# A gated recurrence and a two-branch maximum network: blocks 2 and 3 taken through the seven-product second layer, with the gates and scans of blocks 4 and 5 moved ahead

## The chip, the cores and the metric

The kernel runs on one core of a Trainium2 chip. A core has a matrix engine (TensorE, "PE" in the profile), a vector engine (VectorE, "DVE"), an activation engine (ScalarE, "ACT"), GpSimd ("POOL") and SyncE ("SP"). Each has its own instruction stream, runs it in order, and waits on semaphores for the others. The metric is the device time of one execution in microseconds (us), and lower is better.

## The reference

Four sequences of 6144 steps with 256 channels go through a gated recurrence; its output goes through a layer that takes the larger of two linear maps, and through an output matrix.

```
sig = 1 / (1 + exp(-f_logit))
f = lower_bound + (1 - lower_bound) * sig
i = 1 - f
for t in range(S):                      # S = 6144, batch 4, D = 256
    h = f[:, t] * h + i[:, t] * x[:, t]
    y[:, t] = h
...
h1 = y @ w1                             # 256 -> 1024
h2 = y @ w2
g = maximum(h1, h2)
out = g @ w_out                         # 1024 -> 256, float32
```

The kernel uses max(h1, h2) = h1 + relu(h2 - h1): the first layer is one product with the difference of the weights, and y @ (w1 @ w_out) joins the second layer as two more rows of 128 (the matrix called w13).

## The kernel before

**Tiles.** The 24576 tokens are cut into 48 blocks of 512 (TB), two blocks make a pair p (blocks 2p and 2p+1), so there are 24 pairs (NPAIR). Channels lie on the 128 partitions, in two halves (KC). Blocks 0 to 3 are loaded as they stand and turned on TensorE; from block 4 on, each pair is one chunk of 1024 tokens, which GpSimd's queue casts to 16 bits into a scratch in memory and SyncE's queue reads back transposed (`cross`, L143, which also issues the loads of the next chunk).

**One block's work.** A gate (sigmoid, ACT: L201 for blocks 1 to 3, L279 for the later ones), on DVE the decay (L207), the drive (L217) and two scans (L224), each scan starting from the block before. Then the first layer (`first_layer(j, fc)`, L424): eight groups, fc = 0 to 7, of two matmuls of 512 columns (L434). Two groups fill one dT tile; there are two dT tiles (`ps_d`, bufs=2), and after every second group ACT empties one with a relu into the block's r tiles (L442). These r tiles also hold y.

**Second layer, two forms.** The direct form (`second_layer(j, slot)`, L458) has 40 matmuls of 256 columns a block, issued in eight pieces of five (L480); after every 20 of them a copy (L489) moves the result out of PSUM. The seven-product form (`sevenths(p)`, L517) treats the two blocks of a pair as a 2 by 2 matrix of parts and makes the pair's result out of seven products in place of eight, each of 20 matmuls of 128 columns (L643). Its left sides are r tiles or one of four sums of r tiles (`sum1` to `sum4`, L499, on DVE), its right sides are parts of the output weights or their differences t1 to t4. The products go into PSUM banks called X, B and E; between them a bank is copied into another one (`seed`, L543), saved to memory on chip (`snapshot`, L549), or emptied into the output tile, by an ACT copy (L559) or by a DVE addition with a snapshot (`leave`, L561).

**Order.** It is written out by hand (L657 on), and each engine's stream follows it. Before the change, blocks 0 to 3 use the direct form, and the steps after the start are:

- the first layer of block 2 beside the direct second layer of block 1, one piece a group, with the decay, drive and scans of block 3 in between (L747);
- `cross(6)`; then the first layer of block 3 beside the direct second layer of block 2, with the gates, decays, drives and first scans of blocks 4 and 5 (L762);
- a loop over the pairs from pair 2 (PAIR0) on. It has 16 slots, one first-layer group each. In pair 2, seven slots also take a direct piece of block 3, and one more piece follows in slot 1 of pair 3. From slot 2 of pair 3 (LAG), each slot takes 8.75 of the 140 matmuls (NSEV) of the pair before. The gates of the next pair stand at slots 4, 6, 12 and 14; sums, decays, drives and scans at places counted in ninths of a slot (`seq`).

What is left of the queue follows the loop, and the last pair has a form of its own.

Of the kernel before, what the change touches and what calls it, by code (L numbers as in the profile page):

```python
# [18 lines left out]
def kernel(  # L19
# [10 lines left out]
    nc = tc.nc  # L30

    B, S, D = x.shape
# [6 lines left out]
    LAG = 2  # L39
# [193 lines left out]
    def scan_steps(j):  # L233
        new_mid(j, ("ff", "v"))
        u, ff, v = (mids[j, t] for t in ("u", "ff", "v"))
        new_block(j)
        return [
            lambda: decay(ff, u, slice(0, TB)),
            lambda: drive(v, u, turned[j, 1], slice(0, TB)),
            lambda: scan(j, 0, ff, v, 0),  # L240
            lambda: scan(j, 1, ff, v, 0),
        ]
# [219 lines left out]
    def second_layer(j, slot):  # L462
        ns = TB // P
        n = KC + FC
        total = ns * n
        for k in range(slot * total // FC, (slot + 1) * total // FC):
            i, s = divmod(k, n)
            g, r = divmod(i, 2)
            if s == 0 and r == 0:
                acc["ps"] = ps_o.tile([P, 2, D], FP32, name="ps")  # L470
                if i == 0:
                    acc["osb"] = opool.tile([P, TB // P, D], FP32, name="osb")
            ps, osb = acc["ps"], acc["osb"]
            toks = slice(i * P, (i + 1) * P)
            if s < KC:
                left, right = y_of(j, s)[:, i:TB:ns], w13[:, s, :]
            else:
                fc = s - KC
                left, right = rts[j, fc // KH][:, fc % KH, toks], wob[:, fc, :]
            nc.tensor.matmul(  # L480
                ps[:, r, :],
                lhsT=left,
                rhs=right,
                start=(s == 0 and r == 0),
                stop=(s == n - 1 and r == 1),
                skip_group_check=True,
            )
            if r == 1 and s == n - 1:
                (nc.scalar.copy if j in (0, 3) else nc.vector.tensor_copy)(  # L489
                    out=osb[:, 2 * g : 2 * g + 2, :], in_=ps[:]  # L490
                )
                if i == ns - 1:
                    store(j, osb)
# [17 lines left out]
    def sum1(p):  # L511
        sum_of(p, 1, quarter(p, 1, 0), quarter(p, 1, 1), ALU.add)
# [4 lines left out]
    def sevenths(p):  # L517
# [6 lines left out]
        def product(b, left, w, fresh=False, groups=range(TB // P)):  # L524
            for i in groups:
                for k in range(KH + 1):
                    new = fresh and i == groups[0] and k == 0
                    steps.append([b, left, w(k), i, k, new, None])

        def then(fn):  # L530
            steps[-1][-1] = fn
# [8 lines left out]
        def seed(b, src):  # L540
            def go():
                open_bank(b)
                nc.scalar.copy(out=bank[b][:], in_=bank[src][:])  # L543
            return go
# [8 lines left out]
        def leave(b, j, cols, name, last):  # L553
            def go():
                if j not in osbs:
                    osbs[j] = opool.tile([P, TB // P, D], FP32, name="osb")
                dst = osbs[j][:, :, cols]
                if name is None:
                    nc.scalar.copy(out=dst, in_=bank[b][:])  # L559
                else:  # L560
                    nc.vector.tensor_tensor(  # L561
                        out=dst, in0=bank[b][:], in1=snap[name][:], op=ALU.add
                    )
                if end:
                    store(j, osbs[j], cols=cols)
                elif last:
                    store(j, osbs[j])
            return go
# [25 lines left out]
        def part(t, k2):  # L594
            return lambda: rts[2 * p + t, k2]

        def plain(k2, cols):
            a, b = right(k2, cols)
            return lambda k: a[:, k, :] if k < KH else b

        def given(t):
            return lambda k: t[:, k, :]

        product("X", part(0, 0), plain(0, lo), True)
        then(seed("B", "X"))
        product("E", sub(1), given(t1), True)
        then(snapshot("E", 5))
        if end:
            product("B", part(0, 1), plain(1, lo), groups=range(1))
            product("X", sub(2), given(t2))  # L610
            then(snapshot("X", 2))
            product("B", part(0, 1), plain(1, lo), groups=range(1, 4))
            then(leave("B", ja, lo, None, False))
            product("X", sub(3), given(t3))
            then(leave_both("X"))
            product("E", sub(4), plain(1, hi))
            then(leave("E", ja, hi, 2, True))
            product("X", part(1, 1), given(t4), groups=range(2))
            then(leave_last(slice(0, 2)))
            for i in (2, 3):  # L620
                product("Y", part(1, 1), given(t4), True, groups=range(i, i + 1))
                then(leave_last(slice(i, i + 1)))
        else:
            product("X", sub(2), given(t2))
            then(snapshot("X", 2))
            product("B", part(0, 1), plain(1, lo))
            then(leave("B", ja, lo, None, False))
            product("X", sub(3), given(t3))
            then(leave("X", jb, hi, 5, False))
            product("E", sub(4), plain(1, hi))  # L630
            then(leave("E", ja, hi, 2, True))
            product("X", part(1, 1), given(t4))
            then(leave("X", jb, lo, None, True))
# [23 lines left out]
    with tc.manual_schedule():  # L657
# [85 lines left out]
        turn(turn_steps(3))  # L743
        gate(3)
        cross(5)
        early = scan_steps(3)
        for fc in range(FC):  # L747
            first_layer(2, fc)
            second_layer(1, fc)
            if fc < 4:  # L750
                early[fc]()
        cross(6)
        scans = {PAIR0: pair_scans(PAIR0)}
        gates = {0: 0, 1: 1, 4: 2, 5: 3}
        order = {
            2: ("decay0", "drive0"),
            3: ("scan00",),
            4: ("scan01",),
            6: ("decay1",),
            7: ("drive1",),  # L760
        }
        for fc in range(FC):  # L762
            first_layer(3, fc)
            second_layer(2, fc)
            if fc in gates:
                pair_gate(PAIR0, gates[fc])
            for t in order.get(fc, ()):
                scans[PAIR0][t]()

        queue, due = [], 0  # L770
        pieces3, piece = (1, 3, 5, 9, 11, 13, 15), 0
        for p in range(PAIR0, NPAIR):
            first = p == PAIR0
            more = p + 1 < NPAIR
            seq = [
                (27, scans[p]["scan10"]),
                (36, scans[p]["scan11"]),
                (112, lambda: sum3(p)),
            ]
            if more:  # L780
                scans[p + 1] = pair_scans(p + 1)
                seq += [
                    (64, scans[p + 1]["decay0"]),
                    (66, scans[p + 1]["drive0"]),
                    (70, scans[p + 1]["scan00"]),
                    (84, scans[p + 1]["scan01"]),
                    (131, scans[p + 1]["decay1"]),
                    (133, scans[p + 1]["drive1"]),
                ]
            if not first:  # L790
                seq += [
                    (9, lambda: sum1(p - 1)),
                    (18, lambda: sum2(p - 1)),
                    (50, lambda: sum4(p - 1)),
                ]
                queue += sevenths(p - 1)
            seq.sort(key=lambda e: e[0])
            gates = {4: 0, 6: 1, 12: 2, 14: 3} if more else {}
            for slot in range(2 * FC):
                first_layer(2 * p + slot // FC, slot % FC)  # L800
                if first and slot in pieces3 or p == PAIR0 + 1 and slot == 1:
                    second_layer(2 * PAIR0 - 1, piece)
                    piece += 1
                if p > PAIR0 + 1 or (p == PAIR0 + 1 and slot >= LAG):
                    due += NSEV / (2 * FC)
                    while due >= 1:
                        due -= 1
                        queue.pop(0)()
                if slot == 2 and p + 3 < NPAIR:
                    cross(blocks[2 * p + 6][3])  # L810
                if slot in gates:
                    pair_gate(p + 1, gates[slot])
                while seq and seq[0][0] < (slot + 1) * 9:
                    seq.pop(0)[1]()
# [38 lines left out]
```

## Time and profile before

| | |
|---|---|
| Median of four runs | 378.9 us (378.23 to 379.26) |
| The profiled execution | 379.36 us, of which the span of instructions is 377.6 us |
| Granted TensorE clock in it | 0.998 |
| First layer, L434 | 768 matmuls, mean 379 ns of one |
| Relu evictions, L442 | 192, mean 1023 ns of one |
| Direct second layer, L480 | 160 matmuls of 256 columns, mean 273 ns |
| Seven products, L643 | for 22 pairs, 140 matmuls of 128 columns each, mean 219 ns of one |
| Sums on DVE, L499 | 88, mean 1479 to 1488 ns |
| Copies of the direct form, L489 | 4 on DVE, mean 685 ns; 4 on ACT, mean 588 ns |

Matmuls are pipelined: the mean time of one contains the way through the array, and the distance from one start to the next is shorter. In a timeline, each row gives the start, the time from the first start to the last end of the merged instructions, and the instruction with its output and inputs. The relu evictions, too, overlap a little when they follow each other directly. "Span" is from the first to the last instruction; some time of an execution lies around it.

### The profile page before, as it was taken

The page shows a single profiled execution, that of the slowest core. Times are in us where ns is not written, and L with a number is a line of the kernel's source. Part 1 is how long each engine was busy: PE and PEld are TensorE (multiplying, and loading weights), DVE is VectorE, ACT ScalarE, POOL GpSimd, SP SyncE. Part 2 cuts the span into 40 slices and gives each one's busy share as a digit, 9 for nine tenths or more (in the row PEclk, how much of TensorE's full clock was granted, in tenths as well). Part 3 has the DMA queues.
Part 4 walks back from the last instruction along what each step waited for, and adds up shares of the span by engine and source line. Part 5 has one row for each costly group of instructions (what it writes and reads, how often), then busy time and mean ns, then how long its engine had stood idle before and what let it go on. Part 6 is the DMA issues. An engine that isn't in the chain of part 4 may idle for free.

```text
span 377.6 us, 9634 instructions
## 1 busy us (share of the span) xinstructions
PE 368.3 (98%) x4156; PEld 280.4 (74%) x4156; DVE 338.2 (90%) x408; ACT 303.1 (80%) x412; POOL 41.3 (11%) x80
## 2 busy tenths in 40 slices
PE   7799999999999999999999999999999999999995
PEld 5577767777777777777777777777777777777784
DVE  5696789999999999999999999999999999999762
ACT  5856798888888798888888887987988888888752
POOL 1401101110120201210101101202011101000000
PEclk9999999999999999999999999999999999999999
DMA  7999999999998989989999999899999989960223
GB/s 270 237 194 246 223 166 187 221 231 205 278 182 169 269 147 251 272 165 221 228 191 260 199 193 264 123 242 266 158 240 272 199 200 273 144 249 2 114 113 112
DMA packets 104543, 77.17 MB, mean 204 GB/s; under 512 B 93298, under 2 KB 95348, under 8 KB 103796
## 3 DMA queue, kind: packets, MB, share of 16 engines
q1 hardware_dynamic: 101536, 51.19, 59.8%
q0 software_dynamic: 2544, 25.17, 34.8%
q8 instruction: 32, 0.52, 0.6%
q10 hardware_dynamic: 420, 0.20, 0.2%
q14 instruction: 11, 0.09, 0.1%
HBM read 53.48 MB, written 48.23 MB: 269 GB/s over the span
## 4 chain that ended last, share of the span: by engine, by line
PE 94%; DMA 4%; SPq 0%; POOL 0%; DVE 0%; issue 0%; ACT 0%; DVEq 0%
PE ps L643 45%; PE dT L434 43%; PE ps L480 5%; DMA xT<-in_x_dram 2%; DMA r<-in_moe_w_dram 1%; PE ps L174 1%; SPq L117 0%; POOL wob L666 0%; DVE osb L561 0%; POOL fT L105 0%; DVE osb L582 0%; ACT sn L574 0%; PE dT L643 0%; POOL waited L341 0%; DVEq L561 0%
## 5 line engine op out<-in xcount | busy, mean ns | idle before, releaser
L442 ACT ACTIVATE r<-dT 128x1024 f16<-128x1024 f32 x192 | 195.9, 1023 | 53.5 <-PE dT L434 53.3
L434 PE MATMUL dT<-r,wd 128*128 128x512 f16 x768 | 225.0, 379 | 0.0
L643 PEld LDWEIGHTS <-S 128*128 128x128 f16 x1760 | 115.5, 101 | 37.2 <-DVE S L499 0.2
L643 PEld LDWEIGHTS <-r 128*128 128x128 f16 x1320 | 90.9, 101 | 36.8 <-issue 0.2
L224 DVE TENSOR_TENSOR_SCAN r<-ff,r,v 128x512 f16<-128x512 f16 x88 | 108.2, 1271 | 0.8
L643 PE MATMUL ps<-t,S 128*128 128x128 f16 x1320 | 101.6, 219 | 0.0
L499 DVE TENSOR_TENSOR S<-r 128x2560 f16<-128x2560 f16 x44 | 65.5, 1488 | 15.2 <-ACT r L442 15.2
L434 PEld LDWEIGHTS <-wd 128*128 128x128 f16 x768 | 67.6, 113 | 4.7 <-DVE wd L358 0.2
L643 PE MATMUL ps<-wob,r 128*128 128x128 f16 x704 | 69.9, 219 | 0.0
L499 DVE TENSOR_TENSOR S<-r,S 128x2560 f16<-128x2560 f16 x44 | 65.1, 1479 | 0.0
L279 ACT ACTIVATE u<-fT 128x512 f16<-128x512 f16 x88 | 56.1, 638 | 0.0
L341 POOL CAST waited<-fT 128x1 f32<-128x1 f16 x22 | 15.6, 707 | 278.4 <-DMA fT<-scr 278.4
L207 DVE TENSOR_SCALAR ff<-u,nom 128x512 f16<-128x512 f16 (+1 forms) x98 | 31.8, 347 | 8.5 <-ACT u L201 3.1
L643 PE MATMUL ps<-w,r 128*128 128x128 f16 x176 | 38.5, 219 | 0.0
L643 PE MATMUL ps<-t,r 128*128 128x128 f16 x430 | 34.1, 219 | 0.1
L561 DVE TENSOR_TENSOR osb<-ps,sn 128x512 f32<-128x512 f32 x44 | 30.1, 685 | 3.2 <-PE ps L643 3.2
L643 PE MATMUL ps<-wob,S 128*128 128x128 f16 x352 | 32.6, 219 | 0.0
L217 DVE TENSOR_TENSOR v<-u,xT 128x1024 f16<-128x1024 f16 x44 | 30.2, 686 | 0.0
L549 ACT COPY sn<-ps 128x512 f32<-128x512 f32 x44 | 25.8, 586 | 2.0 <-PE ps L643 2.0
L559 ACT COPY osb<-ps 128x512 f32<-128x512 f32 x43 | 25.1, 583 | 0.8 <-PE ps L643 0.8
L480 PEld LDWEIGHTS <-r 128*128 128x128 f16 x160 | 16.0, 101 | 6.5
L643 PE MATMUL ps<-w,S 128*128 128x128 f16 x88 | 19.3, 219 | 0.0
(58 smaller groups left out, 133.3 us busy)
## 6 DMA issues: line engine op xcount, KB each, us to landing
out_dram<-osb SPq DMA_DIRECT2D x46, 512.0 KB, 3.8
scr<-in_f_logit_dram POOLq DMA_DIRECT2D x22, 512.0 KB, 7.6
scr<-in_x_dram POOLq DMA_DIRECT2D x22, 512.0 KB, 10.3
r<-in_moe_w_dram SPq DMA_DIRECT2D x4, 512.0 KB, 6.4
fT<-in_f_logit_dram POOLq DMA_DIRECT2D x3, 256.0 KB, 8.7
xT<-in_x_dram POOLq DMA_DIRECT2D x3, 256.0 KB, 9.4
out_dram<-osb SPq DMA_DIRECT2D x3, 256.0 KB, 2.5
osb<-in_f_logit_dram SPq DMA_DIRECT2D x2, 256.0 KB, 3.4
```

What stands on the lines that cost most here:

```text
L207: nc.vector.tensor_scalar(out=ff[:, h, cols], in0=u[:, h, cols], scalar1=nom[:, h : h + 1], scalar2=1.0, op0=ALU.mult, op1=ALU.add,)
L217: nc.vector.tensor_tensor(out=like(v[:, :, cols], xT), in0=like(u[:, :, cols], xT), in1=xT, op=ALU.mult,)
L224: nc.vector.tensor_tensor_scan(out=y_of(j, h), data0=ff[:, h, o : o + TB], data1=v[:, h, o : o + TB], initial=0.0 if t0 == 0 else y_of(j - ...
L279: nc.scalar.activation(out=mids[p + NBLK, "u"][:, h, cols], in_=held[c, 0][:, h, cols], func=AF.Sigmoid, scale=-1.0,)
L434: nc.tensor.matmul(dT[:, fc % 2, :], lhsT=wd[:, kc, unit_cols(fc)], rhs=y_of(j, kc), start=(kc == 0), stop=(kc == KC - 1),)
L442: nc.scalar.activation(out=rts[j, k][:, g - 1 : g + 1, :].rearrange("p q (i m) -> p q i m", m=P), in_=dT[:].rearrange("p q (m i) -> p q i ...
L480: nc.tensor.matmul(ps[:, r, :], lhsT=left, rhs=right, start=(s == 0 and r == 0), stop=(s == n - 1 and r == 1), skip_group_check=True,)
L499: nc.vector.tensor_tensor(out=t[:], in0=a, in1=b, op=op)
L549: nc.scalar.copy(out=t[:], in_=bank[b][:])
L559: nc.scalar.copy(out=dst, in_=bank[b][:])
L561: nc.vector.tensor_tensor(out=dst, in0=bank[b][:], in1=snap[name][:], op=ALU.add)
L643: nc.tensor.matmul(bank[b][:, i, :], lhsT=a[:, k, cols], rhs=w, start=fresh, stop=after is not None, skip_group_check=True,)
```

## The change

Blocks 2 and 3 (pair 1) leave the direct form and go through the seven products:

- In the first layer of block 2, the eight direct pieces of block 1 come one group later (so that piece 7 falls into the first layer of block 3), block 3's scans come all ahead of it, and the gates 0 to 2 of pair 2 and its first decay, drive and scans are placed there.
- The first layer of block 3 has that one direct piece, and gate 3 of pair 2. Behind it stand sum 3 of pair 1, and the second decay and drive of pair 2.
- In the pair loop, pair 2 now has the seven products of pair 1 from slot 2 on, and sums 1, 2 and 4 of pair 1. The direct pieces in the loop are gone. In pair 2 alone, gates 0 and 1 of the next pair are one slot later, and its first decay, drive and scans one slot (nine ninths) later.
- For pair 1 alone, product X is not seeded into bank B but saved as a snapshot, bank B is opened afresh by its own product, and the two are added on DVE as B leaves.
- Both copies of block 1's direct form go from DVE to ACT.

```diff
@@ second_layer
             if r == 1 and s == n - 1:
-                (nc.scalar.copy if j in (0, 3) else nc.vector.tensor_copy)(
+                nc.scalar.copy(
                     out=osb[:, 2 * g : 2 * g + 2, :], in_=ps[:]
                 )
@@ sevenths
+        begin = p == PAIR0 - 1
         product("X", part(0, 0), plain(0, lo), True)
-        then(seed("B", "X"))
+        then(snapshot("X", 1) if begin else seed("B", "X"))
         product("E", sub(1), given(t1), True)
...
-            product("B", part(0, 1), plain(1, lo))
-            then(leave("B", ja, lo, None, False))
+            product("B", part(0, 1), plain(1, lo), begin)
+            then(leave("B", ja, lo, 1 if begin else None, False))
@@ the order
         cross(5)
-        early = scan_steps(3)
+        for step in scan_steps(3):
+            step()
+        scans = {PAIR0: pair_scans(PAIR0)}
         for fc in range(FC):
             first_layer(2, fc)
-            second_layer(1, fc)
-            if fc < 4:
-                early[fc]()
+            if fc:
+                second_layer(1, fc - 1)
+            if fc > 4:
+                pair_gate(PAIR0, fc - 5)
+        for t in ("decay0", "drive0", "scan00", "scan01"):
+            scans[PAIR0][t]()
         cross(6)
-        scans = {PAIR0: pair_scans(PAIR0)}
-        gates = {0: 0, 1: 1, 4: 2, 5: 3}
...
         for fc in range(FC):
             first_layer(3, fc)
-            second_layer(2, fc)
-            if fc in gates:
-                pair_gate(PAIR0, gates[fc])
-            for t in order.get(fc, ()):
-                scans[PAIR0][t]()
+            if fc == 1:
+                second_layer(1, 7)
+            if fc == 3:
+                pair_gate(PAIR0, 3)
+        sum3(1)
+        for t in ("decay1", "drive1"):
+            scans[PAIR0][t]()
...
-                    (64, scans[p + 1]["decay0"]),
-                    (66, scans[p + 1]["drive0"]),
-                    (70, scans[p + 1]["scan00"]),
-                    (84, scans[p + 1]["scan01"]),
+                    (73 if first else 64, scans[p + 1]["decay0"]),
+                    (75 if first else 66, scans[p + 1]["drive0"]),
+                    (79 if first else 70, scans[p + 1]["scan00"]),
+                    (93 if first else 84, scans[p + 1]["scan01"]),
...
-            if not first:
-                seq += [
-                    (9, lambda: sum1(p - 1)),
-                    (18, lambda: sum2(p - 1)),
-                    (50, lambda: sum4(p - 1)),
-                ]
-                queue += sevenths(p - 1)
+            seq += [
+                (9, lambda: sum1(p - 1)),
+                (18, lambda: sum2(p - 1)),
+                (50, lambda: sum4(p - 1)),
+            ]
+            queue += sevenths(p - 1)
             seq.sort(key=lambda e: e[0])
-            gates = {4: 0, 6: 1, 12: 2, 14: 3} if more else {}
+            gates = {5 if first else 4: 0, 7 if first else 6: 1, 12: 2, 14: 3}
+            gates = gates if more else {}
             for slot in range(2 * FC):
                 first_layer(2 * p + slot // FC, slot % FC)
-                if first and slot in pieces3 or p == PAIR0 + 1 and slot == 1:
-                    second_layer(2 * PAIR0 - 1, piece)
-                    piece += 1
-                if p > PAIR0 + 1 or (p == PAIR0 + 1 and slot >= LAG):
+                if p > PAIR0 or slot >= LAG:
                     due += NSEV / (2 * FC)
```

More of the change, by code (lines that the diff above doesn't have):

```diff
@@ L745 @@
         cross(5)
-        early = scan_steps(3)
+        for step in scan_steps(3):
+            step()
+        scans = {PAIR0: pair_scans(PAIR0)}
         for fc in range(FC):
             first_layer(2, fc)
-            second_layer(1, fc)
-            if fc < 4:
-                early[fc]()
-        cross(6)
-        scans = {PAIR0: pair_scans(PAIR0)}
-        gates = {0: 0, 1: 1, 4: 2, 5: 3}
[L755 to L761, printed above, removed]
+            if fc:
[4 more added lines that the diff above has]
+            scans[PAIR0][t]()
+        cross(6)
         for fc in range(FC):
             first_layer(3, fc)
-            second_layer(2, fc)
-            if fc in gates:
-                pair_gate(PAIR0, gates[fc])
-            for t in order.get(fc, ()):
-                scans[PAIR0][t]()
+            if fc == 1:
[5 more added lines that the diff above has]
+            scans[PAIR0][t]()
         queue, due = [], 0
-        pieces3, piece = (1, 3, 5, 9, 11, 13, 15), 0
         for p in range(PAIR0, NPAIR):
```

## The prediction

> **What bounds the kernel now.** I read the page first: span, busy shares, the forty slices, then the chain that ended last.
>
> ```profile
> span 377.6 us, 9634 instructions
> PE 368.3 (98%) x4156; PEld 280.4 (74%) x4156; DVE 338.2 (90%) x408; ACT 303.1 (80%) x412; POOL 41.3 (11%) x80
> PE   7799999999999999999999999999999999999995
> PE 94%; DMA 4%; SPq 0%; POOL 0%; DVE 0%; issue 0%; ACT 0%; DVEq 0%
> ```
>
> The chain is TensorE for 94% of the span and DMA (the first loads) for 4%. The timeline of PE has no gap between 19 us and the tail. So every matmul taken out shortens the end by its full pitch, every wait put into PE lengthens it in full, and nothing later gives either back. VectorE (DVE, 90%) and ScalarE (ACT, 80%) are only just covered, so an average says little and I go to the stretch that the change edits: 28.5 us (first layer of block 2) to the end of pair 2. Before 28.5 us nothing moves.
>
> The timeline there, engine by engine (start, duration, instruction): two prices of PE, then the place where PE already runs close behind ACT, then ACT.
>
> ```profile
> 59.06 0.59 PE L434 MATMUL dT<-r,wd 128*128 128x512 f16 x2
> 59.49 0.67 PE L643 MATMUL ps<-t,S 128*128 128x128 f16 x9
> 59.99 0.59 PE L434 MATMUL dT<-r,wd 128*128 128x512 f16 x2
> ...
> 48.40 1.89 PE L434 MATMUL dT<-r,wd 128*128 128x512 f16 x8
> 50.13 0.71 PE L480 MATMUL ps<-wob,r 128*128 128x256 f16 x5
> 50.67 1.03 PE L434 MATMUL dT<-r,wd 128*128 128x512 f16 x4
> ...
> 48.09 1.02 ACT L442 ACTIVATE r<-dT 128x1024 f16<-128x1024 f32 x1
> 48.99 0.63 ACT L279 ACTIVATE u<-fT 128x512 f16<-128x512 f16 x1
> 49.51 1.94 ACT L442 ACTIVATE r<-dT 128x1024 f16<-128x1024 f32 x2
> 51.32 0.60 ACT L489 COPY osb<-ps 128x512 f32<-128x512 f32 x1
> 51.78 1.06 ACT L442 ACTIVATE r<-dT 128x1024 f16<-128x1024 f32 x1
> ```
>
> Starts give the pitch: one first-layer group (2 matmuls) 0.432 us, a seven-product matmul 0.50/9 = 0.0555, a direct piece of 5 matmuls 50.67 - 50.13 = 0.545. On ACT, start to start: relu eviction 0.92 (two in 1.94, one is 1.02), gate 0.52, copy 0.48. A relu starts 0.19 us after its second group's last matmul (the group that ends at 29.95 has its relu at 30.14). A group writes the half of dT that the relu two evictions earlier has emptied: the group starting at 48.40 + 2 x 0.432 = 49.26 needed the relu of 48.09, which ended at 49.11. So PE follows a relu's end within 0.15 us at most; the first weight load behind an ACT cast followed by 0.04 us (cast end 10.12, load at 10.16). I take 0.06.
>
> **Matmuls removed and added.** Removed: blocks 2 and 3 direct, 16 pieces x 0.545 = 8.73 us. Added: 7 x 4 x 5 = 140 matmuls x 0.0555 = 7.77. Gain **0.96 us**. [...] The row above (nine between two groups in 0.50 us, weights loaded each time) decides for 0.0555.
>
> **Fillers moved.** This is where the cost is. Before, each group of blocks 3 and 4-5 had direct pieces beside it; now block 3's eight groups have one piece (the last of block 1), and slots 0 and 1 of pair 2 have nothing. Without filler two groups take 0.86 us and their relu 0.92, so ACT is slower than PE, and a copy (block 1's second eviction, moved from DVE) and gate 3 stand in its queue as well.
>
> PE: group (2,0) at 28.54, then seven times group and piece, 0.977 each, so block 3 starts at 35.81. Groups (3,0), (3,1), piece, (3,2) to (3,5) end at 38.94. Without waits (4,2), slot 2, would start at 40.67.
>
> ACT: relu of (2,6)/(2,7) at 35.52 (behind gates 0 and 1), gate 2 at 36.44, relu (3,0)/(3,1) at 36.96, copy 37.88, relu (3,2)/(3,3) 38.36, gate 3 39.28, relu (3,4)/(3,5) 39.81, relu (3,6)/(3,7) 40.73.
>
> PE waits: (3,6) for the relu ending at 39.38: 39.44 - 38.94 = 0.50. (4,0) for that ending at 40.83: 40.89 against 40.31, 0.58. (4,2) for that ending at 41.75: 0.06. Sum **1.14 us**. Release anywhere from 0.04 to 0.15 moves this sum only to 1.12 or 1.23, since the last wait fixes the position. From slot 2 on 0.5 us of seven-product work stands beside each group and ACT (about 12 us of work in a pair of 14.7) falls back within its cover.
>
> **Gates and scans of blocks 4 and 5.** Gates 0 to 2 move to 34.5 to 37, gate 3 to 39.3; their input landed at 31.2, and that of the drive at 32.8 (issues at 25.29 and 27.78, 5.9 and 5.0 us to landing). No wait. Behind gates 0 and 1 on ACT stands the relu of (2,6)/(2,7), 0.06 late, which nobody on PE needs before 37.2. Scans of block 4 end at 39.1, needed at 40.9. Free.
>
> **Sums and adds on VectorE.** Added: four sums of 1.40 us (pitch), three adds against two for a normal pair (the block's lower half is now an add with a snapshot, 0.60, where it was a copy on ACT). Removed: four copies of 0.60 (two of them to ACT, two for good; block 3's ACT copies go as well). The order on DVE from sum 3 on is what before has one pair later, so I read its time there:
>
> ```profile
> 53.02 1.47 DVE L499 TENSOR_TENSOR S<-r 128x2560 f16<-128x2560 f16 x1
> 54.40 0.78 DVE L207 TENSOR_SCALAR ff<-u,nom 128x512 f16<-128x512 f16 x2
> 55.10 0.69 DVE L217 TENSOR_TENSOR v<-u,xT 128x1024 f16<-128x1024 f16 x1
> 55.74 1.49 DVE L499 TENSOR_TENSOR S<-r 128x2560 f16<-128x2560 f16 x1
> 57.15 1.48 DVE L499 TENSOR_TENSOR S<-r,S 128x2560 f16<-128x2560 f16 x1
> 58.55 2.45 DVE L224 TENSOR_TENSOR_SCAN r<-ff,r,v 128x512 f16<-128x512 f16 x2
> 60.92 1.47 DVE L499 TENSOR_TENSOR S<-r,S 128x2560 f16<-128x2560 f16 x1
> 62.31 0.61 DVE L207 TENSOR_SCALAR ff<-u,nom 128x512 f16<-128x512 f16 x2
> 62.83 0.69 DVE L217 TENSOR_TENSOR v<-u,xT 128x1024 f16<-128x1024 f16 x1
> 63.55 2.46 DVE L224 TENSOR_TENSOR_SCAN r<-ff,r,v 128x512 f16<-128x512 f16 x2
> ```
>
> It has no idle time and takes 12.9 us from sum 3 to the end of the second pair of scans (63.55 + 2.37). Now sum 3 starts at 39.43 (relu (3,2)/(3,3)). Sum 1 starts at about 42.0 and ends 43.5, needed by step 20 at 43.7; sum 2 ends 44.9, needed at 46; block 5's second scan ends 47.24, and the matmul that reads it stands at 47.50. All covered, the last by 0.2 us only. The chain ends at 52.3, then comes the new add (0.60), sum 3 of pair 2 (1.40), and the add that empties bank X (0.69): 55.0, or 54.9 with the second decay at 0.52. Step 120 accumulates into X again. It stands behind slot 0 (40.89) by 16 groups and 120 steps, 6.90 + 6.66 + 0.06: 54.51. So PE waits **0.45 us** for DVE. In before this add ended at 68.33 and its matmul stood at 69.06, because pair 3 had a direct piece (0.545) and no third add. After it, sum 1 of pair 2 is done at 58.0 against 59.2; I find no further wait.
>
> **Queues.** SP issues the transposes for chunk 6 ahead of block 1's store, which then leaves at about 55 rather than 42.3; stores of blocks 2 and 3 go behind chunk 7's transposes. Their output buffers come round only two pairs later: free. If a store held a buffer, an add on DVE would show it. POOL's order is as before, its waits follow the transposes.
>
> **Sum.** -0.96 + 1.14 + 0.45 = **+0.63 us**. The profiled execution took 379.36 us (span 377.6 and 1.76 around it), so 380.0 for it; the median of the runs shown is 0.46 lower, 378.9, so I predict 379.5. About 0.2% (0.76 us) is what a measurement of this kernel tells from no change.
>
> **Rivals.**
> 1. *Full gain.* Relu evictions keep up, only matmuls count: 378.9 - 0.96 = 377.9. For it: ACT is 20% idle and PE shows no gap. Against: its own pitch of 0.92 over 0.86 in a stretch without filler. Chance 0.06.
> 2. *Only ACT bites.* DVE makes up half a microsecond (decays at 0.52[...]), step 120 doesn't wait: +0.18, 379.1. For: bounds of the wait are 0 to 0.6. Chance 0.24.
> 3. *Forecast*, both waits, +0.63: 379.5. Chance 0.39.
> 4. *Slower: DVE becomes the bound of pair 2.* Its 15.5 us from sum 3 to the X add have no idle time. If they run 5% longer, the wait of step 120 is 0.45 + 0.8; from 0.2 us late on, block 5's first group waits already. Price +1.4, 380.3. For: the decays at 54.40 took 0.70 start to start, not 0.52. Against: the sums and scans keep their pitch throughout. Chance 0.28.
> 5. [...]
>
> **Numbers.** Case 3's own range is 379.1 to 380.0. Widened to take in case 2 and most of 4: 378.4 to 380.6. Slower by over 0.2% (above 379.66): case 4 and about 0.4 of case 3, 0.45. Faster (below 378.14): most of case 1, 0.05. Within: 0.50.
>
> **What would show it.** In the changed profile: direct pieces halved (80 rows of 256 columns fewer, 140 of 128 more); PE idle in front of first-layer matmuls, released by the relu eviction, 1.1 us in about three waits near 39 to 42 us; one wait of 0.4 near 54.5 before a product with t4, released by the osb add; slot 0 of pair 2 at 40.9. Wrong if PE is gapless there (case 1), if block 5's first group waits for a scan (case 4), or if waits appear behind 60 us, which I rule out.

## The result and the profile after

The changed kernel takes 379.97 us (median of 44 runs, 378.44 to 382.69), the kernel before 378.93 us (63 runs). The ratio is 1.0023, with a 95% interval of 1.0012 to 1.0033: slower by about 0.87 us, at least 0.45 and at most 1.25. The forecast was +0.63 us, or a median of 379.5. The measured difference is just above the 0.2% that can be told from no change. The profiled execution took 380.11 us.

The page of the changed kernel, parts 1, 2, 4 and 5, gives the first picture:

```profile
span 378.2 us, 9763 instructions
PE 368.1 (97%) x4216; PEld 280.0 (74%) x4216; DVE 342.8 (91%) x411; ACT 305.1 (81%) x416; POOL 39.9 (11%) x80
...
PE   7899999999999999999999999999999999999994
...
PE 88%; DVE 4%; DMA 4%; ACT 2%; issue 1%; SPq 0%; POOL 0%; DVEq 0%
...
L434 PE MATMUL dT<-r,wd 128*128 128x512 f16 x768 | 225.5, 379 | 0.7 <-ACT r L442 0.7
...
L646 PE MATMUL ps<-t,r 128*128 128x128 f16 x450 | 35.7, 219 | 0.3 <-DVE osb L561 0.2
```

PE has 60 matmuls more (80 of 256 columns out, 140 of 128 in), yet its busy time is 0.2 us lower. The chain that ended last, 94% PE before, now passes through DVE and ACT as well. The last two rows name both releasers: the relu evictions in front of first-layer matmuls, and the addition into the output tile in front of a product with t4. (L643 of the kernel before is L646 here; the added lines shift it by three.)

The timeline of PE in the changed kernel shows where. Columns: start, time from first start to last end, instruction; in brackets the idle time ahead and who ended it.

```profile
28.38 1.03 PE L434 MATMUL dT<-r,wd 128*128 128x512 f16 x4
...
36.52 0.71 PE L480 MATMUL ps<-wob,r 128*128 128x256 f16 x5
37.06 1.89 PE L434 MATMUL dT<-r,wd 128*128 128x512 f16 x8
39.27 1.02 PE L434 MATMUL dT<-r,wd 128*128 128x512 f16 x4 [0.32 <-ACT r L442]
40.70 1.51 PE L434 MATMUL dT<-r,wd 128*128 128x512 f16 x6 [0.41 <-ACT r L442]
42.05 0.38 PE L646 MATMUL ps<-wob,r 128*128 128x128 f16 x4
...
54.30 0.22 PE L646 MATMUL ps<-w,S 128*128 128x128 f16 x1
54.69 0.27 PE L646 MATMUL ps<-t,r 128*128 128x128 f16 x2 [0.17 <-DVE osb L561]
...
372.74 0.72 PE L646 MATMUL dT<-t,r 128*128 128x128 f16 x10
```

The bracket counts from the recorded end of the last matmul, on average 379 ns behind its start (219 ns for one of 128 columns), while unhindered starts lie 0.216 us apart (0.0555). So what a wait costs is read from start to start. Group (3,6) should have started at 37.06 + 8 x 0.216 = 38.79 and starts at 39.27: **0.48 us**. Slot 0 should have started at 39.27 + 4 x 0.216 = 40.13 and starts at 40.70: **0.57**. The six matmuls from 40.70 on should end their issue at 42.00, the next row starts at 42.05: **0.05**. The first t4 product should have started at 54.30 + 0.0555 = 54.36 and starts at 54.69: **0.34** by the unrounded times. The sum is 1.44 us.

**The measure of the experiments.** What comes ahead of block 2 hangs on the first loads, which do not end at the same time in each execution. In the chains of before, after and e11 (described below) a load of x ends at 18.43, 18.27 and 18.02 us, and the row that opens block 2's first layer starts 10.1 us later in all three. In the fourteen profiles of this study this row starts between 27.40 and 28.75 us. That is more than the effect. So I count from this row to the last row of products on PE, the *stretch*. Before it is 372.38 - 28.54 = 343.84 us, after 372.74 - 28.38 = 344.36: +0.52. The matmul term of the forecast and the four waits make -0.96 + 1.44 = +0.48.

### The profile page after: what moved, and what is told of

It is laid out like the page before. It is cut to its first block, busy times and chain, and to the rows that moved or that the text cites. A ratio compares the mean times of both kernels' runs of the same rounds, so it can differ in the third digit from the quotient of the medians.

```text
span 378.2 us, 9763 instructions
## 1 busy us (share of the span) xinstructions
PE 368.1 (97%) x4216; PEld 280.0 (74%) x4216; DVE 342.8 (91%) x411; ACT 305.1 (81%) x416; POOL 39.9 (11%) x80
## 4 chain that ended last, share of the span: by engine, by line
PE 88%; DVE 4%; DMA 4%; ACT 2%; issue 1%; SPq 0%; POOL 0%; DVEq 0%
PE ps L646 45%; PE dT L434 40%; DMA xT<-in_x_dram 2%; DVE S L499 2%; PE ps L480 2%; DMA r<-in_moe_w_dram 1%; ACT r L442 1%; DVE r L224 1%; PE ps L174 1%; DVE osb L561 1%; SPq L117 0%; ACT u L279 0%; DVE v L217 0%; DVE ff L207 0%; ACT osb L489 0%
## 5 line engine op out<-in xcount | busy, mean ns | idle before, releaser
L646 PEld LDWEIGHTS <-S 128*128 128x128 f16 x1840 | 120.8, 101 | 39.0 <-DVE S L499 0.2
L646 PEld LDWEIGHTS <-r 128*128 128x128 f16 x1380 | 95.1, 101 | 38.9 <-issue 0.5
L646 PE MATMUL ps<-t,S 128*128 128x128 f16 x1380 | 106.3, 219 | 0.0
L499 DVE TENSOR_TENSOR S<-r 128x2560 f16<-128x2560 f16 x46 | 68.5, 1488 | 15.3 <-ACT r L442 15.3
L646 PE MATMUL ps<-wob,r 128*128 128x128 f16 x736 | 73.1, 219 | 0.0
L499 DVE TENSOR_TENSOR S<-r,S 128x2560 f16<-128x2560 f16 x46 | 68.0, 1479 | 0.0
L646 PE MATMUL ps<-w,r 128*128 128x128 f16 x184 | 40.3, 219 | 0.0
L646 PE MATMUL ps<-t,r 128*128 128x128 f16 x450 | 35.7, 219 | 0.3 <-DVE osb L561 0.2
L561 DVE TENSOR_TENSOR osb<-ps,sn 128x512 f32<-128x512 f32 x47 | 32.2, 685 | 3.2 <-PE ps L646 3.2
L646 PE MATMUL ps<-wob,S 128*128 128x128 f16 x368 | 34.1, 219 | 0.0
L549 ACT COPY sn<-ps 128x512 f32<-128x512 f32 x47 | 27.6, 587 | 2.1 <-PE ps L646 2.0
L646 PE MATMUL ps<-w,S 128*128 128x128 f16 x92 | 20.1, 219 | 0.0
L543 ACT COPY ps<-ps 128x512 f32<-128x512 f32 x22 | 12.5, 570 | 3.4 <-PE ps L646 0.6
```

The lines of the kernel that those rows point to most:

```text
L499: nc.vector.tensor_tensor(out=t[:], in0=a, in1=b, op=op)
L549: nc.scalar.copy(out=t[:], in_=bank[b][:])
L561: nc.vector.tensor_tensor(out=dst, in0=bank[b][:], in1=snap[name][:], op=ALU.add)
L646: nc.tensor.matmul(bank[b][:, i, :], lhsT=a[:, k, cols], rhs=w, start=fresh, stop=after is not None, skip_group_check=True,)
```

## The experiments

All edits are to the changed kernel. "Waits" are PE's, start to start, as above. The fourth column is the stretch less its waits. Two waits of the last pair, 0.18 and 0.29 us, are the same in every row, before included, and are left out. Each ratio is to runs of the kernel before taken beside that kernel (medians 378.67 to 378.93). The four rows marked * leave product X out of a part of the output, as told below.

| kernel | waits, us | stretch, us | less waits | median, us | ratio to before [95%] |
|---|---|---|---|---|---|
| before | none | 343.84 | 343.84 | 378.93 | 1 |
| the change | 0.48, 0.57, 0.05; t4 0.34 | 344.36 | 342.92 | 379.97 | 1.0023 [1.0012, 1.0033] |
| e1_gates_early | 0.48, 0.05, 0.36; t4 0.22 | 344.03 | 342.92 | 379.15 | 1.0012 [0.9995, 1.0029] |
| e2_sum3_late | 0.48, 0.57, 0.05 | 344.03 | 342.93 | 378.98 | 1.0016 [0.9999, 1.0033] |
| e6_gates_sum3 | 0.48, 0.05, 0.36 | 343.81 | 342.92 | 379.57 | 1.0021 [1.0007, 1.0035] |
| e3_fill | scan 0.26, snapshot 0.84 | 344.02 | 342.92 | 379.18 | 1.0011 [0.9998, 1.0025] |
| e4_fill_sum3 | scan 0.26, snapshot 0.84 | 344.02 | 342.92 | 379.28 | 1.0006 [0.9991, 1.0022] |
| e5_fill_split | scan 0.35 | 343.31 | 342.96 | 378.92 | 0.9994 [0.9971, 1.0016] |
| e8_seed_only * | 0.48, 0.57, 0.05 | 344.02 | 342.92 | 379.25 | 1.0008 [0.9995, 1.0021] |
| e12_seed_ps | 0.48, 0.57, 0.05 | 344.03 | 342.93 | 380.07 | 1.0024 [1.0003, 1.0046] |
| e10_seed_bank * | 0.48, 0.57, 0.05; later 0.56, 0.72 | 345.29 | 342.91 | 381.0, one run | not timed in rounds |
| e7_fill_seed * | none | 342.95 | 342.95 | 378.23 | 0.9981 [0.9964, 0.9998] |
| e9_fill_seed_bank * | none | 342.96 | 342.96 | 378.75 | 0.9992 [0.9972, 1.0012] |
| e11_fill_seed_ps | none | 342.96 | 342.96 | 378.17 | 0.9983 [0.9964, 1.0001] |

The third and fourth columns carry the whole account: the thirteen kernels below the first row have the same PE work, 342.91 to 342.96 us, and differ only by waits that their timelines name. The timed medians are coarser: e8 and e12 have the same stretch and waits and medians 0.8 us apart. Verdicts below rest on the trace, with the ratio as a check. The two disagree once: e6 has the stretch of the kernel before, and yet its ratio lies wholly above 1 (1.0007 to 1.0035). With one profile of it, this stays open.

### Gates ahead, sum 3 later: what each wait is made of

The theory (A) was the prediction's account; its rival (B) held that gates in ACT's queue make the relu waits by themselves. e1 moves all four gates of pair 2 ahead of block 3, and the second decay and drive ahead of sum 3:

```diff
-            if fc > 4:
-                pair_gate(PAIR0, fc - 5)
+            if 2 < fc < 7:
+                pair_gate(PAIR0, fc - 3)
@@ the first layer of block 3
-            if fc == 3:
-                pair_gate(PAIR0, 3)
-        sum3(1)
         for t in ("decay1", "drive1"):
             scans[PAIR0][t]()
+        sum3(1)
```

> Edit to the changed kernel: gates 0 to 3 of pair 2 all in the first layer of block 2 (groups 3 to 6), so that no gate stands among block 3's relus, and the second decay and drive of pair 2 ahead of sum 3 on DVE. Unit of account: from the start of block 2's first layer to the start of the last row of products, 343.84 us before and 344.36 changed. Theory A (PE loses 1.1 us to the relus of block 3 and 0.34 to the DVE sequence that starts at sum 3, and that sequence alone fixes when the first t4 product may run): relu waits fall only from 1.10 to about 0.9, since with two dT tiles a pair of groups comes round in 0.86 + 0.19 + 1.02 + 0.05 = 2.12 us per two; slot 2 starts 0.2 earlier; the DVE sequence ends 0.38 earlier, the t4 product waits about 0.17; sum -0.38: 343.98. Rival B (the gate in ACT's queue is what costs, the DVE wait is a fixed 0.34): relu waits fall by a gate's 0.52, sum -0.5: 343.85. Rival C (the loss lies outside this stretch, in products, stores or transposes): no change, 344.36.

PE of e1, the same stretch of its timeline:

```profile
37.43 1.89 PE L434 MATMUL dT<-r,wd 128*128 128x512 f16 x8
39.64 1.94 PE L434 MATMUL dT<-r,wd 128*128 128x512 f16 x8 [0.32 <-ACT r L442]
41.77 0.59 PE L434 MATMUL dT<-r,wd 128*128 128x512 f16 x2 [0.20 <-ACT r L442]
```

The first wait stays (37.43 + 1.73 = 39.16 against 39.64: 0.48), and 0.41 of the rest stays (39.64 + 1.73 = 41.37 against 41.77). Gate 3 was worth 0.21 of 1.10 us. What remains is the round trip of a dT tile. The timeline of ACT in the changed kernel:

```profile
36.78 1.03 ACT L442 ACTIVATE r<-dT 128x1024 f16<-128x1024 f32 x1
37.70 0.59 ACT L489 COPY osb<-ps 128x512 f32<-128x512 f32 x1
38.16 1.05 ACT L442 ACTIVATE r<-dT 128x1024 f16<-128x1024 f32 x1
39.08 0.66 ACT L279 ACTIVATE u<-fT 128x512 f16<-128x512 f16 x1
39.60 1.97 ACT L442 ACTIVATE r<-dT 128x1024 f16<-128x1024 f32 x2
```

Groups (3,2) and (3,3) fill a tile until 37.06 + 0.86 = 37.92. Their relu may start 0.19 later, at 38.11; it starts at 38.16, so the copy ahead of it delays it by 0.05. It ends at 39.21, and PE writes that tile again at 39.27. Meanwhile PE has only two more groups (0.86 us) to do. With two tiles and nothing between the groups, an estimate from these rows is that a tile comes round after 0.86 + 0.19 + 1.02 + 0.05 = 2.12 us, and PE fills two in 1.73: it must wait 0.39 in each round, even with an empty ACT. The rows of ACT in e1 show such a round:

```profile
38.53 1.97 ACT L442 ACTIVATE r<-dT 128x1024 f16<-128x1024 f32 x2
40.70 1.94 ACT L442 ACTIVATE r<-dT 128x1024 f16<-128x1024 f32 x2 [0.20 <-PE dT L434]
```

No gate and no copy stands here, and ACT itself is idle for 0.20 us. Group (3,6) starts at 39.64 and group (4,2), two tiles later, at 41.77: 2.13 us.

e2 puts sum 3 of pair 2 behind the addition that empties X:

```diff
-                (112, lambda: sum3(p)),
+                (118 if first else 112, lambda: sum3(p)),
```

> Edit to the changed kernel: in pair 2 alone, sum 3 of the pair itself stands one slot later, behind the addition that empties X, with nothing else moved. Theory A: that addition starts 1.4 us earlier, about 52.6, and the t4 product near 54.4 doesn't wait; the relu waits stay at 1.10; sum -0.34: 344.02, and the kernel is within 0.1% of the one before. Rival B (DVE has too much work in this pair in whichever order): the wait comes back within a slot or two at another product or scan, 344.36. Rival C: 344.36, with the wait gone and time lost elsewhere.

DVE of the changed kernel, then DVE and PE of e2, by their timelines:

```profile
39.25 1.49 DVE L499 TENSOR_TENSOR S<-r 128x2560 f16<-128x2560 f16 x1 [0.30 <-ACT r L442]
40.66 0.61 DVE L207 TENSOR_SCALAR ff<-u,nom 128x512 f16<-128x512 f16 x2
41.18 0.69 DVE L217 TENSOR_TENSOR v<-u,xT 128x1024 f16<-128x1024 f16 x1
...
48.34 0.62 DVE L207 TENSOR_SCALAR ff<-u,nom 128x512 f16<-128x512 f16 x2
48.87 0.69 DVE L217 TENSOR_TENSOR v<-u,xT 128x1024 f16<-128x1024 f16 x1
49.59 2.46 DVE L224 TENSOR_TENSOR_SCAN r<-ff,r,v 128x512 f16<-128x512 f16 x2
51.97 0.67 DVE L561 TENSOR_TENSOR osb<-ps,sn 128x512 f32<-128x512 f32 x1
52.55 1.49 DVE L499 TENSOR_TENSOR S<-r 128x2560 f16<-128x2560 f16 x1
53.95 0.69 DVE L561 TENSOR_TENSOR osb<-ps,sn 128x512 f32<-128x512 f32 x1
```

```profile
51.19 1.36 DVE L561 TENSOR_TENSOR osb<-ps,sn 128x512 f32<-128x512 f32 x2
52.47 1.48 DVE L499 TENSOR_TENSOR S<-r 128x2560 f16<-128x2560 f16 x1
```

```profile
53.52 0.22 PE L646 MATMUL ps<-w,S 128*128 128x128 f16 x1
53.58 0.28 PE L646 MATMUL ps<-t,r 128*128 128x128 f16 x2
```

In e2 both additions stand ahead of the sum and end at 52.55, a microsecond before t4 is due; the t4 product follows 0.06 us after the matmul ahead of it. The wait is gone and the stretch is 0.33 us shorter. No other wait came in its place.

e6 joins both edits:

> Edit to the changed kernel: the first two edits together (gates 0 to 3 early with the second decay and drive ahead of sum 3; sum 3 of pair 2 one slot later), no filler among block 3's groups. Theory A: relu waits 0.89 as with the gates alone, no wait ahead of the t4 product: 343.84 - 0.96 + 0.89 = 343.77, level with the kernel before, which is what the missing filler alone costs against the matmuls saved. A rival, that DVE caps the pair: 344.0 as with either edit alone.

The stretch is 343.81, which is that of the kernel before: order alone takes back 0.55 of the 1.44 us. The 0.89 that is left are the three waits for relus of e1, with the copy's 0.05 in them.

### Products into the empty groups

e3 spreads product X of pair 1 over block 3's groups. It also puts product B ahead of E, leaves the addition of B to a fixed place on DVE, and takes the remaining steps of pair 1 at a lower rate:

```diff
@@ sevenths
+        if begin:
+            product("B", part(0, 1), plain(1, lo), True)
+            then(lambda: None)
+            late.append(leave("B", ja, lo, 1, False))
         product("E", sub(1), given(t1), True)
...
-            product("B", part(0, 1), plain(1, lo), begin)
-            then(leave("B", ja, lo, 1 if begin else None, False))
+            if not begin:
+                product("B", part(0, 1), plain(1, lo))
+                then(leave("B", ja, lo, None, False))
@@ the first layer of block 3
+        queue, due = sevenths(1), 0
...
+            for _ in range((0, 0, 0, 4, 2, 4, 1, 8)[fc]):
+                queue.pop(0)()
@@ the pair loop
-            queue += sevenths(p - 1)
+            if not first:
+                queue += sevenths(p - 1)
+            else:
+                seq.append((46, late[0]))
...
+                if first and slot == 0:
+                    queue.pop(0)()
...
-                    due += NSEV / (2 * FC)
+                    due += (102.5 / 14) if first else NSEV / (2 * FC)
```

> Edit to the changed kernel: product X of pair 1 (20 matmuls, 1.11 us, needing block 2's r tiles only) is issued among block 3's groups and slot 0 of pair 2, where PE waits; product B follows in the loop before E, the rate in pair 2 is 7.32 a slot so that as much is left over as before, and B's addition stands behind block 5's scans. The same work is done. Theory A: relu waits fall from 1.10 to about 0.1 since useful work fills them, slot 2 still starts at 42.0, but the DVE sequence is no earlier, so the wait ahead of the first t4 product grows from 0.34 to about 1.1 to 1.4: sum about 0, 344.36. Rival B (PE's waits for relus are the loss, and filling them gains them): -1.0, 343.35. Rival C: 344.36 with the t4 wait as it was and time lost elsewhere.

Both theories missed: 344.02. The relu waits and the t4 wait are gone, but two others stand in their place, seen in the timelines of PE and of ACT of e3:

```profile
48.45 0.27 PE L652 MATMUL ps<-t,S 128*128 128x128 f16 x2
49.39 0.44 PE L652 MATMUL ps<-t,S 128*128 128x128 f16 x5 [0.67 <-ACT sn L550]
```

```profile
48.76 0.59 ACT L550 COPY sn<-ps 128x512 f32<-128x512 f32 x1
```

With B out of the way, the two products of X stand next to each other, and between them ACT, which a relu holds until then, must save the bank: 48.76 + 0.59 = 49.35, and PE goes on at 49.39, 0.84 late. In the changed kernel product B lies between and hides it. A further 0.26 goes to block 5's first group, which waits for its scan. I had priced the filler and not what B's old place had covered.

e4 is e3 with e2's line:

> Edit: both the last two edits (X among block 3's groups, and sum 3 of pair 2 one slot later). Theory A: neither the relus nor the X addition hold PE up in pair 2, 1.1 + 0.34 us come free; DVE, without idle time since sum 3, then gives some 0.5 back in pair 3 (sum 1, block 7's scans, the X addition, 0.1 to 0.3 each): about -0.6 to -0.9 against the changed kernel, 343.5 to 343.8, equal to or just below the kernel before. Rival B: all is gained, -1.4: 342.9. Rival C: 344.36.

It too missed: 344.02, with the same two waits. In e3 the addition of X already stood ahead of sum 3, so e2's line had nothing to move.

e5 joins the gates of e1, sum 3 of e2 and the filler, and cuts B in two instead of moving it, half ahead of E and half in its old place:

```diff
+        if begin:
+            product("B", part(0, 1), plain(1, lo), True, range(2))
         product("E", sub(1), given(t1), True)
...
-            product("B", part(0, 1), plain(1, lo), begin)
+            product("B", part(0, 1), plain(1, lo), groups=range(2 * begin, 4))
```

> Edit to the changed kernel: gates 0 to 3 in the first layer of block 2 and the second decay and drive ahead of sum 3, product X of pair 1 among block 3's groups and in slot 0, sum 3 of pair 2 one slot later; and product B cut in two, ten matmuls ahead of E and ten between the second and third product in X, so that the snapshot of X has work beside it on PE. The same work is done. Theory A: no relu wait (filled), no wait for block 5's scan (DVE sequence 0.35 earlier, 0.26 was missing), the wait for the snapshot falls from 0.84 to between 0 and 0.4, some 0.1 given back in pair 3: from the start of block 2's first layer to the last row of products 343.84 - 0.96 + 0.1 to 0.5 = 343.0 to 343.4, so 0.1 to 0.2% below the kernel before. A rival, that DVE's total work caps pairs 2 and 3 whatever the order: the waits come back at scans and sums of pair 3, 343.8 to 344.0.

One wait is left, in the timeline of PE of e5, for a scan of block 7:

```profile
60.09 0.38 PE L434 MATMUL dT<-r,wd 128*128 128x512 f16 x1
60.66 0.38 PE L434 MATMUL dT<-r,wd 128*128 128x512 f16 x1 [0.19 <-DVE r L224]
```

60.09 + 0.216 = 60.31 against 60.66: 0.35. The stretch, 343.31, lies in the range of theory A, but the wait stands where its rival put it, at a scan of pair 3. This is the mechanism of rival 4 of the prediction, DVE as the bound of the pair, but only once PE runs earlier. The third addition, the new one of bank B with the snapshot, takes DVE about 0.6 us (51.97 to 52.55 in the changed kernel).

### Without the third addition

e7 is e5 with pair 1 seeded like every other pair: ACT copies X into B, B leaves by an ACT copy, and DVE has two additions. e8 is the changed kernel with this alone.

```diff
-        then(snapshot("X", 1) if begin else seed("B", "X"))
+        then(seed("B", "X"))
...
-            then(leave("B", ja, lo, 1 if begin else None, False))
+            then(leave("B", ja, lo, None, False))
```

> Edit to the kernel of the run with product B cut in two: pair 1 seeds bank B from X by an ACT copy as all other pairs do, so that B leaves by an ACT copy and DVE has two additions in pair 2 instead of three. Theory A (the one wait left, 0.35 us at pair 3's slot 8 for block 7's second scan, is the DVE sequence running without idle time since sum 1; an addition of 0.60 less in it removes the wait): no wait in front of a scan, 343.84 - 0.96 + 0 to 0.1 = 342.9 to 343.0 from the start of block 2's first layer to the last row of products, 0.9 less than before, a ratio of about 0.9977. The seed's ACT copy ends when B's first matmul comes up (41.3 against 41.4), so 0 to 0.1 there. A rival (the wait there is set by sum 2 and the scans' own place in the order): 0.35 stays, 343.3.

> Edit to the changed kernel alone: pair 1 seeds bank B from X as all other pairs do (no snapshot of X, no third addition on DVE). Theory A (the third addition, 0.60 us ahead of the one that empties X, is what makes the first t4 product wait): wait gone, relu waits stay at 1.10, 344.02. A rival (the wait comes from the late start of sum 3, and the addition only adds to it): with 0.60 less the addition ends at about 54.0 against a product at 54.4, so the same; the two part only if sum 3 of pair 2 were waiting for its relu, when less than 0.34 comes back: 344.1 to 344.3.

e7 has no wait at all and a stretch of 342.95. In e8 the t4 wait goes, as it did in e2 by order alone, and the three relu waits stay. In e7 to e10 the lower half of block 2 (its output columns 0 to 127) lacks product X: the seed is not in the sum that leaves B. The whole output is off by a relative 0.0878 in all four, and leaving this one product out of the reference gives the same 0.0878. The order and the amount of work are not touched by that.

e9 and e10 open E's bank ahead of B's, e9 in e7 and e10 in e8, to give B another bank:

```diff
+                if begin:
+                    open_bank("E")
...
-                if fresh:
+                if fresh and not (begin and b == "E"):
```

> Edit to the kernel with X among block 3's groups and the seed: E takes its PSUM bank before B does, so that B's bank is the one of block 1's direct form (every column last written by matmuls) and not one last written by transposes. [...] with this bank the seeded sum is whole, and the order of work is the same as in the run with the seed, so no wait of PE in the stretch, 343.84 - 0.96 = 342.9, ratio 0.9970 to 0.9990. A rival (the seed is lost for another reason[...]): the output of block 2's lower half is off by the product X as it was.

> The same exchange of banks in the changed kernel with the seed alone: the time of the seed alone, 344.02 from the start of block 2's first layer to the last row of products, relu waits 1.10 and no wait ahead of the first t4 product; output whole by the first theory, off by the product X by the rival.

e9 has the stretch of e7 within 0.01 us, and B still got the bank that the last transposes of block 3's input had used. e10 was run once and is open: its stretch is 345.29 with the waits of e8 and two more, 0.56 us at 172.95 and 0.72 at 232.56, each for an addition on DVE. The addition at 232 us stood 1.3 us behind an output store; for the one at 172 us, idle for 1.1, the profile names PE. The view of waits of e10 from 170 to 235 us has the row (total, times, longest):

```profile
DVE osb L563 <- DMA out_dram<-osb: 1.3, 1, 1.3
```

e8 and e12, with nearly the same order of work, show no such wait. The cause is open; a repeat was not made.

e11 and e12 put B of pair 1 into the bank that block 1's second direct half has left, e11 in e7 and e12 in e8. With it the seed holds and the output has every product again:

```diff
-                open_bank(b)
+                if begin:
+                    t = acc["ps"][:]
+                    bank[b] = t.rearrange("p r (h d) -> p (r h) d", d=P)
+                else:
+                    open_bank(b)
```

> Edit to the kernel with X among block 3's groups and the seed: pair 1's bank B is the PSUM bank of block 1's second direct half itself, every column of which was last written by matmuls; in the run that only exchanged the order of the two banks the pool still gave B the bank of the last transposes. Theory[...]: the seeded sum is whole; order and times as in the run with the seed, no wait of PE in pairs 1 to 3, 343.84 - 0.96 + 0.07 = 342.95 from the start of block 2's first layer to the last row of products, ratio 0.9970 to 0.9990. A rival (the seed is lost for another reason): the output lacks X as before.

> The changed kernel with the third addition alone undone (pair 1 seeds bank B, in the bank of block 1's second direct half). Theory A: relu waits 1.10, no wait ahead of the first t4 product: 344.02, so 0.34 less than the changed kernel and 0.18 more than before. Rival (another reader of PSUM or ACT's extra copy at B's end costs the same): 344.36.

The page and the timeline of PE of e11:

```profile
span 376.7 us, 9764 instructions
...
PE 367.5 (98%) x4216; PEld 281.2 (75%) x4216; DVE 341.6 (91%) x410; ACT 305.8 (81%) x417; POOL 38.3 (10%) x80
```

```profile
28.12 1.03 PE L434 MATMUL dT<-r,wd 128*128 128x512 f16 x4
...
37.67 0.39 PE L652 MATMUL ps<-wob,r 128*128 128x128 f16 x4
37.90 0.59 PE L434 MATMUL dT<-r,wd 128*128 128x512 f16 x2
...
40.23 0.39 PE L652 MATMUL ps<-wob,r 128*128 128x128 f16 x4
40.46 0.59 PE L434 MATMUL dT<-r,wd 128*128 128x512 f16 x2
40.95 1.03 PE L434 MATMUL dT<-r,wd 128*128 128x512 f16 x4
41.82 0.38 PE L652 MATMUL ps<-wob,r 128*128 128x128 f16 x4
...
371.08 0.72 PE L652 MATMUL dT<-t,r 128*128 128x128 f16 x10
```

Products stand between the groups, and no row shown has a bracket. The stretch is 371.08 - 28.12 = 342.96: 0.88 us below the kernel before and 1.40 below the change. The timed ratio is 0.9983 with an interval of 0.9964 to 1.0001; the gain that the trace shows would be 0.9977. The timing alone does not quite separate it from no gain. e12 has the stretch of e8. DVE and PE of e12 where the t4 wait was:

```profile
52.37 0.68 DVE L565 TENSOR_TENSOR osb<-ps,sn 128x512 f32<-128x512 f32 x1
...
53.32 0.22 PE L650 MATMUL ps<-w,S 128*128 128x128 f16 x1
53.38 0.27 PE L650 MATMUL ps<-t,r 128*128 128x128 f16 x2
```

The addition that empties X ends at 53.05, and the t4 product follows the matmul ahead of it by 0.06.

## Why the prediction was right, step by step

**Matmuls, -0.96.** Right. Stretches less waits lie 0.88 to 0.93 us below the kernel before, in all thirteen kernels of the table. The price of 0.0555 us, read from a row with nine of the 128-column matmuls in 0.50 us, held for all 140.

**Relu waits, +1.14.** Right in size and place: 0.48, 0.57 and 0.05 against 0.50, 0.58 and 0.06. The reason given in words was incomplete: it named ACT's pitch of 0.92 against 0.86 and the copy and gate in its queue. e1 shows that gate 3 makes only 0.21 of it; the larger part is the round trip of two tiles (2.13 us in e1 against 1.73 of filling), which the arithmetic contained and the words left out.

**The wait of the t4 product, +0.45.** Right in mechanism, too large by 0.11; this is the one mis-sized term. From sum 3 to the end of the addition that empties X the forecast had 15.5 us; the rows give 39.25 to 54.64, 15.4. Most of the 0.11 is a slip in the forecast's own sum. It allowed for a second decay of 0.52 us in place of 0.70, and the decay did take 41.18 - 40.66 = 0.52; but 52.3 + 0.60 + 1.40 + 0.69 - 0.18 is 54.8, not 54.9, and the wait then 0.36. Three separate edits confirm the place: without the third addition (e8, e12) or with the addition that empties X ahead of sum 3 (e2), the whole wait goes.

**Gates, scans, queues at nothing; no wait behind 60 us.** Right for the changed kernel. Block 1's store left at 54.78 us and no output buffer came late; the stores of blocks 2 and 3 left at 66.82.

**The sum.** Forecast +0.63, by the trace +0.52, by the timing +0.87 (0.45 to 1.25). The two do not contradict each other, and the timing cannot say more. The measured median, 379.97, is 0.47 above the 379.5 of the forecast and just inside the 379.1 to 380.0 of its case 3.

**Rivals.** The full gain (rival 1) needs all four waits gone; only e7, e9 and e11 have that, and of these only e11 has the whole output. Rival 2, no wait at step 120, is refuted for the change and is what e2, e8 and e12 became. Rival 4, DVE as the bound, did not come: the wait was 0.34, and block 5's first group did not wait. It appeared when e3 and e5 had removed PE's own waits (0.26 and 0.35), so the cover was as thin as the prediction said.

**Not tried.** A third dT tile might shorten the round trip; a dT tile (128x1024 f32 in the rows of ACT) is as large as two of the products' tiles (128x512 f32), and whether there is room for a third was not shown. Nor was DVE work given to GpSimd.

## What to carry to other kernels

When a change takes work out of the groups that another engine empties, price the round trip of the buffer (fill, start of the eviction, eviction, return), not only the pitch of the two engines: here 0.9 us fewer matmuls bought 1.1 us of such waits, and filling the groups again took all of them away, moving the gates only 0.2. Before moving a filler elsewhere, ask what its old place covered (e3 lost 0.84 us to a snapshot that product B had hidden). For effects below 1 us, count from a fixed instruction in the trace and subtract the named waits; the remainder must then be the same in every variant with the same matmuls.

## What was not expected of the hardware

**A seed held in one bank and not in another.** In e11 and e12, ACT copies X into a bank that the direct form's matmuls wrote last, the matmuls of B follow without the start flag, and the output holds both products. In e7 to e10 the same steps go to a bank that the 16-bit transposes of block 3's input wrote last, and the output lacks X (relative error 0.0878). e8 and e12 differ in the choice of this bank alone. Nor is it a property of that one bank: in e8 the later pairs seed the same bank, after products have filled it, and lose nothing, since block 2's X accounts for the whole 0.0878. Why the seed is lost there, no run shows. So the snapshot and the third addition of pair 1, which at their place cost the 0.34 us, stand in for a bank that holds the seed; in e12 another bank does it without that wait.

**The jitter of the start.** The first row of block 2's first layer moved by 1.35 us between profiles (27.40 to 28.75). In three of them it stands 10.1 us behind the end of a load of x, as told above; what set it in the others was not shown. The range is more than twice the 0.52 us of the change's own effect in the trace.
